# Order of v loads, partition groups and index scatters in an attention and mixture-of-experts kernel

## The chip, the cores and the metric

One core of one Trainium2 chip runs the whole program. The metric is the device time of one execution in microseconds, and lower is better.

## The reference

Two layers in a row. The attention takes q, k and v of 8 batches, 8 heads, 576 positions and 64 dimensions. It adds two softmax attentions: one over q, k and v averaged over groups of 4 positions (144 by 144 scores), its output repeated 4 times, and a local one in which a position sees the 3 before and the 3 behind it. The result, as 4608 tokens of 512 numbers, goes through a mixture of 8 experts, each token through the one with the largest gate:

```
logits = x @ w_gate + modality_bias[modality_id]
e_idx = np.argmax(logits, axis=1)
...
gate_w = probs[np.arange(N), e_idx]
for e in range(E):
    mask = e_idx == e
    h = np.maximum(x[mask] @ w1[e], 0.0)
    out[mask] = gate_w[mask, None] * (h @ w2[e])
```

## The kernel before, in words

**Attention.** It runs in N = 32 steps; step n does the heads 2·(n mod 4) and the next of batch n // 4. The order is a software pipeline written out by hand: a table PHASE gives each piece of work a place in steps, `call(n + p, ...)` collects all of them, and they are recorded in the order of these numbers. Each engine then works in that order (a piece that waits holds up all that stands behind it on its engine). In one step TensorE turns q and k (`tp`, L296), scores them (`sc` L364, `scd` L390), averages v (`vp` L284, once for two steps, so on one half of a batch's v), and multiplies by v (`avd` L460, `avl` L475). GpSimd (POOL) adds up q (`qe` L342, `qd` L346), adds a small number to the sums (`z` L412) and scales the two attention matrices (`le` L420, `de` L424); `scd` waits for `qd`, `avl` for `le` by way of a transposition (`lt`, L431) and a copy (`Pw`, L436).

**Loads.** All plain transfers are issued by SyncE (SP), in the same recorded order. A half batch of q and k is 4 transfers over 128 partitions (L252). A half batch of v is 4 transfers of 30 partitions each, one for each 32-partition group, in the order 0, 2, 1, 3 (L272; the last batch is cut once more, L271). v has two buffers, `vw` of even and of odd batches; a half of one is free when the products `avl` of the batch two before have read it. In before both halves of the next batch but one step are recorded together at 4·b − 1 + P["v"] and 0.8 steps later.

**Routing.** Nine or ten half tiles of tokens of a batch are turned back (`R`) and stored to a scratch `xs` in DRAM (`store`, L647): 4 transfers, one for each 32-partition group, in the order 0 to 3. Each token's place in its expert's list is worked out on VectorE (`pb` ends with the column `si`), and `st` (L653) writes 128 tokens' entries into the table `tab` with one indirect transfer from POOL; a batch has 4 or 5. Batches 0 to 3 (EB = 4) are "early": the first units of 512 tokens for the experts are made from them while the attention still runs. In before each scatter of batches 0 to 6 has a place of its own in the order, those of batch 6 by a rule of their own; those of batch 7 stand behind the attention.

**Experts.** Tokens are gathered by the table (L949, L957). w1 comes in chunks (`fetch`): for w1 4 transfers of 32 partitions and 128 KB each in the order 0 to 3 (L864), for w2 one of 128 partitions (L867). Chunks 0 to 3 of the first expert are loaded and split into a high and a low part while the attention ends: POOL casts chunk 0 and 1 (L888), at ws00 and ws10 of the table, between `z` and `qd` of two late steps, and chunks 2 and 3 behind the last `de`. Behind the attention come two units of 512 tokens, three of 1024, and three small ones; TensorE's float32 products in three passes (L1026, L1079) fill it from then on.

**A scheduler for what is not written out.** The pieces in `manual_schedule()` keep their order. Those recorded outside of it, as batch 7's routing under `high_priority()`, are put by a scheduler where it holds them to be ready, and that can be between pieces recorded earlier.

Of the kernel before, what the change touches and what calls it, by code (L numbers as in the profile page):

```python
# [23 lines left out]
B, H, S, D = 8, 8, 576, 64  # L24
# [18 lines left out]
EB = 4  # L43
# [42 lines left out]
def whole(pieces):  # L86

    while True:
        try:
            next(pieces)  # L90
        except StopIteration as x:
            return x.value
# [399 lines left out]
class Router:  # L492
# [147 lines left out]
    def store(s, b, t):  # L640

        n = min(2, s.t["G", b] - 2 * t)
        if n > 0:
            r0 = 128 * (s.t["t0", b] + 2 * t)
            R = s.t.pop(("R", b, t))
            for a in range(4):
                s.nc.sync.dma_start(s.xs[r0 : r0 + 128 * n, 128 * a : 128 * a + 128].rearrange("(i j) x -> j i x", j=32),  # L647
                                    R[32 * a : 32 * a + 32, : 4 * n].rearrange("p i k c -> p i (k c)"))

# [169 lines left out]
class Moe:  # L819
# [38 lines left out]
    def fetch(s, raw, e, c, quarters=False):  # L858
        nc = s.nc
        if c < 4:  # L860
            for i in range(4):
                x, y = (c, i) if quarters else (i, c)
                r = 256 * (x // 2) + 64 * (x % 2) + 128 * (y // 2) + 32 * (y % 2)
                nc.sync.dma_start(raw[32 * i : 32 * i + 32], s.w1[bass.ds(e, 1), r : r + 32, :].rearrange("o p f -> (o p) f"))  # L864
        else:
            c -= 4
            nc.sync.dma_start(raw.rearrange("p (f d) -> p f d", f=2),  # L867
                              s.w2[bass.ds(e, 1), 256 * c : 256 * c + 256, :].rearrange("o (f p) d -> p (o f) d", p=128))
# [226 lines left out]
class Large:  # L1095
# [69 lines left out]
    def first(s, hook):  # L1165
# [20 lines left out]
        for n, nm in enumerate("1256743"):  # L1186
            (wh, wl), (xh, xl) = s.t.pop((nm, "W")), s.t.pop((nm, "X"))
            acc, new = (Z, nm != "3") if nm in "253" else (X, nm == "1")
            for f in range(4):
                fs = slice(128 * f, 128 * f + 128)  # L1190
                for k in range(2):
                    for i, (a, x) in enumerate(((wh, xh), (wh, xl), (wl, xh))):
                        nc.tensor.matmul(acc[f], a[:, k, fs], x[:, k, :], start=new and k == i == 0, stop=k == 1 and i == 2,
                                         skip_group_check=True)
                t = X[f]
                if nm == "6":
                    if f == 0:
                        part = m.block("raw1", F32).rearrange("p (f t) -> p f t", f=4)
                    nc.scalar.copy(part[:, f], t)
                elif nm in "273":  # L1200
                    t = m.xp.tile([128, DM], F32, name="o", bufs=3)
                    if nm != "3":
                        nc.scalar.copy(t, X[f])
                    nc.vector.tensor_tensor(t, part[:, f] if nm == "3" else t, Z[f], op=ALU.add)  # L1204
                if late:
                    store(*late.pop())
                if nm in "2743":
                    late.append(({"2": 0, "7": 6, "4": 2, "3": 4}[nm], f, t))
                hook(n, f)
        store(*late.pop())  # L1210
        s.h = [[[H[i + j] for j in (0, 2)] for i in (0, 1)], [[H[i + j] for j in (4, 6)] for i in (0, 1)]]

# [5 lines left out]
def build(tc, q, k, v, mid, w_gate, bias, w1, w2, out):  # L1218
    nc = tc.nc
    with ExitStack() as ctx:  # L1220
# [10 lines left out]
        with ExitStack() as actx:  # L1231
            ectx = ExitStack()
            ro = Router(tc, ctx, C, ps, xs, tab, tables)
# [5 lines left out]
            at = Attention(tc, actx, ectx, C, ps, q, k, v)  # L1239
# [9 lines left out]
            N = 4 * B  # L1249
# [17 lines left out]
            def call(at, f, *args):  # L1267
                calls.append((at, len(calls), f, args))

            P = PHASE  # L1270
            parts = {"kT": "kT_", "Pw": "Pw_", "W": "store", "lm": "lm", "le": "le"}
            used = max(P["avl0"], P["avl1"])
# [3 lines left out]
            for nm, p in P.items():  # L1276
                if nm in FIXED or nm[:2] in SETUP:
                    continue
                f, i = (nm[:-1], int(nm[-1])) if nm[-1].isdigit() else (nm, 0)
                if f in batch:  # L1280
                    for b in range(B - 1):
                        at_ = 4 * b + p
                        if f == "st" and b == B - 2:
                            at_ = {2: max(N - 2 + P["nd"], 4 * b + P["pb"]) + 0.0001, 0: N - 1 + P["nl"] + 0.0001,
                                   3: N - 0.865 + P["nd"]}.get(i, N + 2.2)
                        call(at_, getattr(ro, parts.get(f, f)), b, i)
                else:
                    for n in range(0, N, 2 if f in ("vp", "vc", "tpt") or nm in ("qT1", "kT1", "kd1") else 1):
                        call(n + p, values if f == "X" else getattr(at, parts.get(f, f)), n, i)
            for b in range(B):  # L1290
                if b + 1 < B:
                    for j in range(2):
                        call(4 * b - 1 + P["v"] + 0.8 * j, at.load_v, b + 1, 4 * j)
            for h in range(3, N // 2):
                call(2 * h - 5 + P["qk"], at.load_qk, h // 2, h % 2)

# [57 lines left out]
            t = 4 * (EB - 1) + max(P[x] for x in P if x[:2] == "st") + 0.02  # L1354
# [7 lines left out]
                call(sorted(P[f"row{j}"] for j in range(4))[i], rows, 0, i)  # L1362
            free = N - 1 + max(P["scd"], P["sc0"], P["sc1"]) + 0.02

            w = max(t + 5, 4 * (B - 2) - 1 + used + 1.1 + 0.8)
            for c in range(4):
                call(w - 1.5 + 0.5 * c, wload, c)
            for c in range(2):
# [29 lines left out]
            b = B - 1  # L1398
            with tc.high_priority():
                for f, k in ((ro.lg, 2), (ro.LT, 2), (ro.lgt, 2), (ro.L, 2)):  # L1400
                    for i in range(k):
                        f(b, i)
                for f in ROUTE[:9] + ROUTE[10:12]:
                    getattr(ro, f)(b, 0)
                cnt = whole(ro.counts("m"))
                for f in ("pr", "pa", "pb"):
                    getattr(ro, f)(b, 0)
                for i in range(5):
                    ro.st(b, i)
            moe.after = ro.last_act, ro.last_dve  # L1410
            for i in range(5):
                ro.R(b, i)
# [7 lines left out]
        lists, Es, Ts, Rs, Xs, parts = {}, {}, {}, {}, {}, {}  # L1420

        N, written = len(order), ExitStack()
# [208 lines left out]
```

## Time and profile before

| | us |
|---|---|
| median of 3 runs | 677.1 (673.7 to 679.29) |
| the profiled execution | 672.38 |
| its span, first to last instruction | 670.7 |
| TensorE busy in the span | 633.4 |

The profile is of one execution. TensorE's busy share is a share of the span, with ends that are modelled; VectorE is DVE, ScalarE is ACT, GpSimd is POOL, SyncE's queue is SPq. In a timeline the brackets give the idle time of the engine ahead of an instruction and what ended it. [...]

### The profile page before, as it was taken

How to read it: one execution, taken by the hardware profiler on the slowest of the kernel's cores; microseconds unless marked ns; L12 is line 12 of the kernel's file. 1: busy time of each engine (PE TensorE's matmuls, PEld its weight loads, DVE VectorE, ACT ScalarE, POOL GpSimd, SP SyncE). 2: the span in 40 equal slices, each digit the busy share in tenths (PEclk: the TensorE clock that was granted, in tenths of full speed). 3: DMA queues.
4: the chain of work that ended last, by engine and by line, in shares of the span. 5: the costliest groups of instructions: out<-in, count | busy, mean ns of one | idle time of the engine just before them, and what ended most of it. 6: DMA issues, size and time to landing. Idle time of an engine off the chain costs nothing. (4 is left out here: it accounts for less than half of the span.)

```text
span 670.7 us, 16185 instructions
## 1 busy us (share of the span) xinstructions
PE 633.4 (94%) x5995; PEld 498.4 (74%) x5995; DVE 425.6 (63%) x897; ACT 386.8 (58%) x902; POOL 345.7 (52%) x414
## 2 busy tenths in 40 slices
PE   7799999899988769999999999999999999999996
PEld 4577677676756556887888888888888888889894
DVE  6678898699968574834435773676736967225550
ACT  4789999899979462413354743446424464335540
POOL 7635666557656665333039876498764740113102
PEclk9899999899989797999999999999999999999999
DMA  9999988997999968077002326233351244537701
GB/s 184 163 168 194 160 152 180 161 203 146 177 176 184 190 159 211 27 186 194 0 33 98 107 74 175 53 103 103 84 158 72 79 111 141 169 113 212 233 1 44
DMA packets 178011, 90.20 MB, mean 134 GB/s; under 512 B 144036, under 2 KB 162506, under 8 KB 177930
## 3 DMA queue, kind: packets, MB, share of 16 engines
q1 hardware_dynamic: 169994, 69.96, 49.0%
q0 software_dynamic: 7936, 19.18, 9.3%
q8 instruction: 48, 0.79, 0.6%
q14 instruction: 33, 0.27, 0.2%
HBM read 69.86 MB, written 19.51 MB: 133 GB/s over the span
## 5 line engine op out<-in xcount | busy, mean ns | idle before, releaser
L1079 PE MATMUL l<-V,H 128*128 128x512 f32 x804 | 190.4, 395 | 0.0
L1079 PEld LDWEIGHTS l<-V,H 128*128 128x128 f32 x804 | 150.3, 188 | 34.6
L957 POOL DMA_INDIRECT xg<-xs,m x64 | 74.7, 1167 | 19.2 <-issue 18.9
L1089 POOL DMA_INDIRECT out_dram<-o,tq x24 | 28.9, 1204 | 79.4 <-ACT o L1081 61.4
L1026 PE MATMUL l<-X,H 128*128 128x512 f32 (+1 forms) x264 | 58.8, 374 | 0.9 <-DVE X L999 0.9
L436 ACT COPY Pw<-lt 32x288 f32<-32x288 f32 x128 | 54.5, 426 | 5.3 <-DVE lt L431 3.8
L1081 ACT ACTIVATE o<-l,tq 128x512 f32<-128x512 f32 x24 | 16.5, 689 | 70.1 <-PE l L1079 45.1
L1026 PEld LDWEIGHTS l<-X,H 128*128 128x128 f32 x264 | 45.4, 192 | 10.9 <-issue 1.5
L653 POOL DMA_INDIRECT tab<-ig,si x36 | 38.4, 1066 | 15.5 <-DVE mhni L677 9.4
L475 PE MATMUL avl<-Pw,vw 128*64 128x96 f32 x768 | 42.3, 257 | 4.2 <-ACT Od L465 2.0
L1182 ACT ACTIVATE H<-o 128x512 fp32r<-128x512 f32 x36 | 22.8, 634 | 39.8 <-DVE o L1204 39.6
L1089 POOL DMA_INDIRECT out_dram<-o,tg x12 | 14.0, 1170 | 59.8 <-ACT o L1081 43.1
L412 POOL TENSOR_SCALAR z<-z 128x15 f32<-128x15 f32 x32 | 8.4, 261 | 68.0 <-ACT de L403 22.5
L475 PEld LDWEIGHTS avl<-Pw,vw 128*64 128x64 f32 x768 | 34.4, 141 | 9.9 <-ACT Od L465 3.7
L1031 ACT ACTIVATE H<-l 128x512 fp32r<-128x512 f32 x24 | 14.4, 599 | 46.9 <-PE l L1026 46.9
L328 ACT COPY kT<-tp 64x512 f32<-64x512 f32 x64 | 37.0, 578 | 4.4 <-DVE kd L336 2.8
L894 DVE TENSOR_TENSOR V<-raw,V 128x1024 fp32r<-128x1024 f32 x23 | 34.3, 1509 | 7.4 <-ACT V L888 7.4
L364 PE MATMUL sc<-kT,qT 128*24 128x64 f32 x1536 | 35.2, 223 | 3.7 <-ACT kT L328 3.3
L403 ACT ACTIVATE de<-scd,dm 128x144 f32<-128x144 f32 x96 | 35.6, 373 | 3.3 <-DVE dm L395 2.4
L894 DVE TENSOR_TENSOR H<-raw,H 128x1024 fp32r<-128x1024 f32 x12 | 15.0, 1256 | 34.5 <-ACT H L888 19.4
L1032 DVE SCALAR_TENSOR_TENSOR H<-l,H 128x512 fp32r<-128x512 f32 x24 | 16.6, 690 | 30.5 <-ACT H L1031 30.4
L390 PE MATMUL scd<-kd,qd 64*64 64x144 f32 x384 | 32.7, 306 | 1.0 <-POOL qd L346 1.0
(276 smaller groups left out, 1450.5 us busy)
## 6 DMA issues: line engine op xcount, KB each, us to landing
raw<-in_moe_w_dram SPq DMA_DIRECT2D x112, 128.0 KB
raw<-in_moe_w_dram SPq DMA_DIRECT2D x28, 512.0 KB
vw<-in_v_dram SPq DMA_DIRECT2D x60, 180.0 KB
qt<-in_q_dram SPq DMA_DIRECT2D x30, 288.0 KB
kt<-in_k_dram SPq DMA_DIRECT2D x30, 288.0 KB
xs<-R SPq DMA_DIRECT2D x56, 128.0 KB
xs<-G SPq DMA_DIRECT2D x8, 128.0 KB
xg<-xs,m POOLq DMA_INDIRECT x64, 2.9
```

Source lines behind the costliest of these rows:

```text
L328: s.nc.scalar.copy(s.kB[r, g, a, PAD + 64 * g : PAD + 64 * g + 512], p[r])
L364: s.nc.tensor.matmul(p[32 * j : 32 * j + SUB, 2 * i : 2 * i + 2, :], qT[:, q0 : q0 + SUB], kB[:, :, q0 : q0 + WIN], start=False, stop=(i = ...
L390: s.nc.tensor.matmul(p[r, c, :], qd[r, 40 * c : 40 * c + 64], kd[r, :], start=True, stop=True, skip_group_check=True)
L403: s.nc.scalar.activation(x, s.t["scd", n][:, c].rearrange("p (k x) -> p k x", k=NB), AF.Exp, bias=m[:, c : c + 1], accum_out=s.t["z", n][: ...
L436: s.nc.scalar.copy(s.Pw[n % NPW][r, :, j, :SUB], s.t["lt", n][r, :, :SUB])
L475: s.nc.tensor.matmul(p[64 * a : 64 * a + 64, c], vw[:, NB * (4 * (hp // 2) + hp % 2 + 2 * a) + k, :], Pw[:, 2 * k + a], start=True, stop=T ...
L653: i = nc.gpsimd.indirect_dma_start(out=s.tab[:, :], out_offset=bass.IndirectOffsetOnAxis(ap=C.si[:, t : t + 1], axis=0), in_=C.ig[:, t, :] ...
L894: (nc.gpsimd if turn == 4 else nc.vector).tensor_tensor(lo, raw, hi.bitcast(F32), op=ALU.subtract)
L957: s.nc.gpsimd.indirect_dma_start(out=R[l].rearrange("p h (i x) -> p (h i) x", i=4)[:, i, :], out_offset=None, in_=s.xs.rearrange("n (a x) ...
L1026: nc.tensor.matmul(p[:, f % n, :], a[:, fs], x[:, k, :N], start=(k == 0 and i == 0), stop=(k == 3 and i == 2))
L1079: nc.tensor.matmul(p, l, x[:, f % 2, :], start=(f == 0 and i == 0), stop=(f == 7 and i == 2))
L1089: nc.gpsimd.indirect_dma_start(out=s.out[:, :], out_offset=bass.IndirectOffsetOnAxis(ap=T[:, h, 0:1], axis=0), in_=o, in_offset=None, boun ...
```

## The change

Three edits. `store` and `fetch` go through the groups in the order 0, 2, 1, 3. Scatters of batches 4 to 6 lose their places in the order and are recorded behind the attention with those of batch 7, under `high_priority()`. The halves of v are recorded apart, each 0.02 steps behind the last reader of its buffer (`used` is the later of avl0 and avl1), which is 2.2 steps earlier for the first half and 1 step earlier for the second; the place `w` of the first weights is 0.3 steps earlier.

```diff
-            for a in range(4):
+            for a in (0, 2, 1, 3):
                 s.nc.sync.dma_start(s.xs[r0 : r0 + 128 * n, 128 * a : 128 * a + 128].rearrange("(i j) x -> j i x", j=32),
...
-            for i in range(4):
+            for i in (0, 2, 1, 3):
                 x, y = (c, i) if quarters else (i, c)
...
                     for b in range(B - 1):
-                        at_ = 4 * b + p
-                        if f == "st" and b == B - 2:
-                            at_ = {2: max(N - 2 + P["nd"], 4 * b + P["pb"]) + 0.0001, 0: N - 1 + P["nl"] + 0.0001,
-                                   3: N - 0.865 + P["nd"]}.get(i, N + 2.2)
-                        call(at_, getattr(ro, parts.get(f, f)), b, i)
+                        if f != "st" or b < EB:
+                            call(4 * b + p, getattr(ro, parts.get(f, f)), b, i)
...
-                        call(4 * b - 1 + P["v"] + 0.8 * j, at.load_v, b + 1, 4 * j)
+                        call(4 * b - 3 + used + 2 * j + 0.02 if b else P["v"] + 0.8 * j - 1, at.load_v, b + 1, 4 * j)
...
-            w = max(t + 5, 4 * (B - 2) - 1 + used + 1.1 + 0.8)
+            w = max(t + 5, 4 * (B - 2) - 1 + used + 1.6)
...
-                for i in range(5):
-                    ro.st(b, i)
+                for x in range(EB, B):
+                    for i in range(5):
+                        ro.st(x, i)
```

On SP, in the middle of the attention (batches 4 and 5; `qt` and `kt` a half of q and k, `vw` v, `xs<-R` a store). Before:

```order
L252 DMA qt<-in_q_dram 128x9x64 x2
L252 DMA kt<-in_k_dram 128x9x64 x2
L647 DMA xs<-R 32x8x128 x4
L272 DMA vw_155<-in_v_dram 30x24x64 x8
L252 DMA qt<-in_q_dram 128x9x64 x2
L252 DMA kt<-in_k_dram 128x9x64 x2
L647 DMA xs<-R 32x8x128 x4
L252 DMA qt<-in_q_dram 128x9x64 x2
L252 DMA kt<-in_k_dram 128x9x64 x2
L647 DMA xs<-R 32x8x128 x4
L272 DMA vw_156<-in_v_dram 30x24x64 x8
```

After, the same stretch:

```order
L272 DMA vw_155<-in_v_dram 30x24x64 x4
L252 DMA qt<-in_q_dram 128x9x64 x2
L252 DMA kt<-in_k_dram 128x9x64 x2
L647 DMA xs<-R 32x8x128 x4
L272 DMA vw_155<-in_v_dram 30x24x64 x4
L252 DMA qt<-in_q_dram 128x9x64 x2
L252 DMA kt<-in_k_dram 128x9x64 x2
L647 DMA xs<-R 32x8x128 x4
L272 DMA vw_156<-in_v_dram 30x24x64 x4
L252 DMA qt<-in_q_dram 128x9x64 x2
L252 DMA kt<-in_k_dram 128x9x64 x2
L647 DMA xs<-R 32x8x128 x4
```

The first half of a batch's v has moved ahead of one half of q and k and one store; the second half stands where it stood.

On SP, at the last batch, from its second half of q and k on (`raw` is chunk 0 of the first expert's w1, four transfers of it to a chunk). Before:

```order
L252 DMA qt<-in_q_dram 128x9x64 x2
L252 DMA kt<-in_k_dram 128x9x64 x2
L647 DMA xs<-R 32x8x128 x4
L272 DMA vw_156<-in_v_dram 30x24x64 x4
L864 ISA
L864 DMA raw_4138<-in_moe_w_dram 32x1024
L864 ISA
L864 DMA raw_4138<-in_moe_w_dram 32x1024
```

After:

```order
L252 DMA qt<-in_q_dram 128x9x64 x2
L252 DMA kt<-in_k_dram 128x9x64 x2
L647 DMA xs<-R 32x8x128 x4
L272 DMA vw_156<-in_v_dram 30x24x64
L271 DMA vw_156<-in_v_dram 30x64
L272 DMA vw_156<-in_v_dram 30x23x64
L271 DMA vw_156<-in_v_dram 30x64
L272 DMA vw_156<-in_v_dram 30x23x64
L271 DMA vw_156<-in_v_dram 27x64
L272 DMA vw_156<-in_v_dram 30x23x64
L864 ISA
L864 DMA raw_4102<-in_moe_w_dram 32x1024
```

The first half of the last v has gone from here to a place ahead of these rows, and the second half, which stood behind chunks 0 and 1, now stands ahead of chunk 0.

On POOL, at the scatters of batch 5 (`L653`), from the first of them on; `L949` is a gather for the first unit, `L888` the cast of chunk 0. Before:

```order
L653 DMA tab<-ig,si 41472x2
L342 TENSOR_TENSOR qe<-qT 128x288
L653 DMA tab<-ig,si 41472x2
L949 DMA xg<-xs,tg_3674 128x512
L412 TENSOR_SCALAR z<-z 128x5x3
L346 TENSOR_TENSOR qd<-qe 128x144
L420 TENSOR_TENSOR le_168<-le_168,zr 128x12x30
L653 DMA tab<-ig,si 41472x2
L424 TENSOR_TENSOR de_171<-de_171,zr 128x18x24
L653 DMA tab<-ig,si 41472x2
L342 TENSOR_TENSOR qe<-qT 128x288
L412 TENSOR_SCALAR z<-z 128x5x3
```

After:

```order
L653 DMA tab<-ig,si 41472x2 x5
L342 TENSOR_TENSOR qe<-qT 128x288
L949 DMA xg<-xs,tg_3674 128x512
L412 TENSOR_SCALAR z<-z 128x5x3
L346 TENSOR_TENSOR qd<-qe 128x144
L420 TENSOR_TENSOR le_168<-le_168,zr 128x12x30
L424 TENSOR_TENSOR de_171<-de_171,zr 128x18x24
L342 TENSOR_TENSOR qe<-qT 128x288
L412 TENSOR_SCALAR z<-z 128x5x3
L888 CAST H_4602<-raw_4102 128x1024
L346 TENSOR_TENSOR qd<-qe 128x144
```

The scheduler has put the five scatters of batch 5 in one run into the attention, where the first of them stood. Batch 4's four stand in the same way in one run where its first one stood, and batch 6's four in one run behind the last `de` but one, where its first one stood; only batch 7's five stand behind the attention, as before.

## Rows read from the trace of the kernel before

**Rows 1.** The page: granted clock and DMA share in 40 slices
```profile
PEclk9899999899989797999999999999999999999999
DMA  9999988997999968077002326233351244537701
```

**Rows 2.** Windows by stage: stretch, length, busy time by engine, clock, DMA share, GB/s
```profile
45.00:223.00 178.00, 164.08 (x3140) 121.15 (x3138) 144.70 (x440) 158.67 (x500) 105.39 (x160) 0.98 0.93 174
223.00:258.00 35.00, 28.40 (x415) 20.90 (x413) 26.41 (x64) 20.92 (x64) 24.75 (x27) 0.84 0.80 165
258.00:661.00 403.00, 402.06 (x1888) 329.66 (x1887) 224.36 (x307) 176.74 (x250) 188.07 (x163) 1.00 0.39 112
```

**Rows 3.** Timeline of TensorE where it waits for v, start, length, idle before
```profile
128.58 1.70 PE L284 MATMUL vp<-vw,pool 128*32 128x256 f32 x12 [1.91 <-DMA vw<-in_v_dram]
...
187.03 1.93 PE L284 MATMUL vp<-vw,pool 128*32 128x256 f32 x12 [3.11 <-DMA vw<-in_v_dram]
...
221.15 1.93 PE L284 MATMUL vp<-vw,pool 128*32 128x256 f32 x12 [5.37 <-DMA vw<-in_v_dram]
...
224.83 1.71 PE L390 MATMUL scd<-kd,qd 64*64 64x144 f32 x12 [0.59 <-POOL qd L346]
```

**Rows 4.** Timeline of SP's queue, 150 to 226 us
```profile
176.86 10.18 SPq L272 DMA_DIRECT2D vw<-in_v_dram  x8
...
209.37 6.70 SPq L272 DMA_DIRECT2D vw<-in_v_dram  x4
216.27 5.04 SPq L864 DMA_DIRECT2D raw<-in_moe_w_dram  x8
221.56 0.35 SPq L272 DMA_DIRECT2D vw<-in_v_dram  x1
...
225.29 0.34 SPq L272 DMA_DIRECT2D vw<-in_v_dram  x1
```

**Rows 5.** Timeline of POOL, batches 4 and 5's scatters and the cast of chunk 0
```profile
172.84 1.06 POOL L653 DMA_INDIRECT tab<-ig,si  x1 [0.16 <-DVE lm L371]
...
185.27 1.05 POOL L653 DMA_INDIRECT tab<-ig,si  x1 [0.15 <-ACT qT L314]
...
204.78 1.10 POOL L653 DMA_INDIRECT tab<-ig,si  x1 [0.16 <-DVE lm L371]
...
213.09 1.01 POOL L653 DMA_INDIRECT tab<-ig,si  x1 [0.17 <-issue]
...
214.90 0.26 POOL L412 TENSOR_SCALAR z<-z 128x15 f32<-128x15 f32 x1
223.34 1.04 POOL L888 CAST H<-raw 128x1024 fp32r<-128x1024 f32 x1 [8.19 <-DMA raw<-in_moe_w_dram]
```

**Rows 6.** Windows as in rows 2, of short stretches
```profile
45.00:62.00 17.00, 17.00 (x344) 12.57 (x344) 15.24 (x51) 16.48 (x55) 8.41 (x15) 1.00 1.11 197
...
149.00:157.00 8.00, 7.00 (x132) 5.31 (x125) 7.87 (x21) 7.10 (x24) 5.92 (x11) 1.00 0.67 113
290.00:292.00 2.00, 2.00 (x10) 1.64 (x9) 0.19 (x1) 0.00 (x0) 0.99 (x1) 1.00 0.79 238
303.00:305.00 2.00, 2.00 (x10) 1.63 (x9) 1.37 (x2) 1.42 (x2) 1.67 (x2) 1.00 1.06 396
...
218.01:234.78 16.77, 13.04 (x177) 8.82 (x179) 9.74 (x22) 8.03 (x25) 11.01 (x13) 0.80 1.10 190
```

**Rows 7.** The table's scatters, 145 to 157 us, and landing of those of 160 to 217 us
```profile
L653 POOL DMA_INDIRECT tab<-ig,si x4: 1004/1028/1054, 145.7 to 153.9; - x4
...
DMA to landing us min/median/max: 5.6/6.1/8.9
```

**Rows 8.** SP's stores of 70 to 215 us: duration min, median, max, first, last
```profile
L647 SPq DMA_DIRECT2D xs<-R x48: 430/479/2475, 74.5 to 207.8; - x48
```

**Rows 9.** Timeline of the attention's end: POOL, ACT, TensorE
```profile
246.62 1.04 POOL L888 CAST H<-raw 128x1024 fp32r<-128x1024 f32 x1
...
250.22 1.09 PE L981 MATMUL xt<-ident,xg 128*128 128x128 f32 x8 [2.94 <-ACT PdT L453]
```

## The prediction

> **What bounds the kernel now.** I read the windows by stage first. From 258 us to the end TensorE is busy 402 of 403 us at full clock [rows 2], and the change alters none of its products there. So the end moves as the start of that stretch moves, and only the attention ahead of it can win or lose time. There the page's slices show the DMA engines at nine tenths or more almost all the way to 235 us [rows 1], a share of 0.93 from 45 to 223 us [rows 2]. TensorE is busy 164 of those 178 us. Two limits lie close together, so I asked next where TensorE stops. Three times it waits for v, ahead of the averages of batches 4, 6 and 7: 1.91, 3.11 and 5.37 us, together 10.4 us [rows 3]. Around the third the granted clock is 0.80 on the mean of 16.77 us [rows 6]; with levels of 1.00 and 0.50 that is 6.7 us at half clock, 3.4 us of work. The page's slices dip at the two before as well [rows 1].
>
> SP's own timeline says why v is late. SP issues without a pause, and a transfer's issue takes about as long as its data: the eight of v for batch 6 take 10.18 us from 176.86 us, and TensorE gets the first four at 187.03 us [rows 4, 3]. The four of batch 7 start at 209.37 us, are issued by 216.07 us and let TensorE go at 221.15 us, 5.1 us later. So the queue stands about 5 us deep behind SP: it is the queue's total content, not the moment at which SP is allowed to issue, that decides when something lands.
>
> The last thing that the queue makes wait is chunk 0 of the weights. POOL is ready for its cast from 215.2 us on and starts it at 223.34 us, after 8.19 us for the raw weights [rows 5]. `qd` stands behind that cast, and TensorE's `scd` at 224.83 us behind `qd` [rows 3]. Everything from there to 258 us is one chain of steps.
>
> **Part 1, halves of v.** By the order, the first half of v of each batch goes ahead of one half of q and k and one store. It then lands some 8 to 10 us earlier, by SP's rows two groups of transfers, and that covers 1.91, 3.11 and 5.37 us. No byte is added or taken away, so what was overtaken lands later: an odd half of q and k moves back by a half of v, 4 to 6 us. I expect some of the waits for v to come back as waits for q and k at `tp`. What matters for the end is chunk 0. Before, the second half of the last v stood behind chunks 0 and 1; now it stands ahead. Its seven transfers took from 221.56 to 225.63 us [rows 4], so chunk 0 lands **4.1 us** later if the queue moves as it did. The 5.37 us wait goes, but TensorE then waits at `scd` a few instructions later, for POOL, which waits for chunk 0: the stall changes its name. `w`'s 0.3 steps hide behind a queue that is late anyway: nothing.
>
> **Part 2, scatters.** The text puts them behind the attention, but the order shows runs of four, five and four inside it. What they cost the queue: from 45 to 62 us, without one, it moves 197 GB/s; from 149 to 157 us, among the four scatters of 145.7 to 153.9 us, 113 GB/s [rows 6, 7]. That is 3.4 us lost of 8, 0.85 us for each. The fifth scatter of batch 5 now runs ahead of chunk 0: +0.9 us, if the loss goes by their number. If it goes by the time in which any is on its way, 6.1 us each [rows 7], the runs win: batch 4's were on their way from 172.84 to 191.4 us and batch 5's from 204.78 to 219.2 us [rows 5]; in runs at 1.2 us each (1.05 and a gap of 0.16) these are 9.7 and 10.9 us instead of 18.5 and 14.4, so 12.3 us less at 43% loss, −5.3 us. Bounds −5.3 and +0.9; I take **−2.0**, the middle, since no row has scatters so close beside loads.
>
> On POOL the run of five holds up `qe`, `z` and `qd` of its step: five times 1.2 us where two scatters stood, about 4 us late. At this place POOL waited 8.19 us for chunk 0 in the next step [rows 5], and that wait is the cover: nothing, or 4 us if chunk 0 came early. The run of four for batch 4 delays its step by about 2 us in the stretch in which the queue is late: nothing. The last run stands ahead of the last step's `z` and `de`, where one scatter stood ahead of `z` and one between `le` and `de`: 4.8 us from the same start instead of 1.2, of which `z` had 1.6 us of idle; by `de` the delay is 1.0 us. The cast of chunk 2 at 246.62 us and TensorE's 2.94 us wait ahead of 250.22 us [rows 9] move with it: **+1.1 us**, between 0 and 2.2 (the delay of `z`).
>
> **Part 3, the groups.** 48 stores of 74.5 to 207.8 us carry 5.8 MB (40 of 128 KB, 8 of 64 KB) [rows 8]. Weights in groups of 32 partitions in the old order move at 238 GB/s, weights over 128 partitions at 396 [rows 6]. If the new order gave stores the second rate for the first, they would take 14.6 us of the queue instead of 24.2: −9.6 us. If groups stay one behind the other, nothing. v, which has the order 0, 2, 1, 3 already, goes at 145 GB/s (8 times 180 KB in 10.18 us) [rows 4], so the order alone brings no high rate; I take **−2.5**, a quarter. Chunk 0's 512 KB: −0.9 to 0 by the same rates, I take **−0.2**.
>
> [...] No row here shows stores in the new order.
>
> **The sum.** Chunk 0: 4.1 − 2.0 − 2.5 − 0.2 = −0.6 us; the end of the attention +1.1. Together **+0.5 us**, no change that can be told. The profiled execution goes from 672.4 to 672.9 us; it lies 4.7 us under the median of the runs, so the median goes from 677.1 to about 678. Steps of 1% (6.8 us) are about what a measurement of this kernel can tell from no change.
>
> **Rivals.**
> Faster: the queue really moves faster. For it speak the two rates of rows 6 and the loss beside scatters; against it the share of 0.93, which leaves little idle, and v's rate. With −9.6 for the stores and −2.0 for the runs, chunk 0 would be 8 us early. The gain ends where v and POOL's own order end it: the 5.37 and 0.59 us waits and 3.4 us of clock, so −9.4, and +1.1 at the end: 664 us, 669 as a median. [...]
>
> Slower: chunk 0 behind the last v. Place: POOL's cast of chunk 0, with `qd` behind it and TensorE behind that. Price: 4.1 us, 0.9 us for the fifth scatter, 1.1 us at the end, and up to 1.7 us, half of the 3.4, for a longer half clock: +7.8, so 680 us, 685 as a median. It decides as soon as neither stores nor runs relieve the queue. Rows 5 speak for it, 8.19 us in which chunk 0 was the last to come; against it, that nothing of the queue's content has been added.
>
> Also possible: the waits for v were the true limit and chunk 0 comes as early as they allow, because TensorE's progress and not the queue holds back SP. Then 10.4 us and at least 3.4 us of clock go: 659 us. Rows 4 speak against it: SP is late, not waiting. I count it with the faster case.
>
> **How the numbers follow.** Forecast, within a few us of 678: 0.52. Faster: 0.26, with a few of its outcomes within 1%. Slower: 0.22, about half at over 1%, and from the forecast's own upper end (+4.1 without relief) some more. This gives faster by over 1% 0.25, within 1% 0.53, slower by over 1% 0.22. The range 666 to 688 reaches from the faster rival's end, a little beyond, to somewhat past the slower one; the likeliest case's own is 673 to 683.
>
> **What would show it.** Right: the waits at `vp` for v are gone or under 1 us; POOL's wait for the raw weights is still there, at some 8 to 12 us, with its cast within 3 us of 223; waits for `qt` or `kt` at `tp` of late steps; DMA share near 0.93 up to the cast. Wrong: a cast before 217 us, or a GB/s clearly above 174 from 45 us to the cast (stores or runs relieved the queue); a cast past 227 us; idle time of TensorE at `scd` of the run of five, which would mean that its 4 us have no cover.

## The result, and the profile after

The changed kernel takes 682.58 us in the median of 20 executions (678.84 to 691.54), the kernel before 675.96 us beside it (20 executions, 671.35 to 685.71). The ratio is 1.0107, with a 95% interval of 1.0082 to 1.0132: it is about 7 us slower. The ratio leaves out executions more than 1.5% above the fastest of their kernel (one of after, three of before), which is why it gives 7.2 us and the medians 6.6. The two profiled executions lie 12.1 us apart (684.50 and 672.38 us), since before's is 3.6 us under its median and after's 1.9 us over its own; the traces therefore show about 5 us more than there is to explain.

TensorE's granted clock (in tenths of full speed) and the DMA share of after, in 40 slices of the page, answer to [rows 1]:

```profile
PEclk9899999998998897999999999999999999999999
DMA  9989788889999943449103226214162233536701
```

The clock dips in other slices than before, the last time (7) at the end of the attention as before, and the DMA engines are busy for seven tenths or more up to the fourteenth slice. The windows of after (stretch, length, busy time by engine, clock, DMA share, GB/s), to be held against [rows 2]:

```profile
45.00:223.00 178.00, 165.51 (x3067) 121.98 (x3055) 142.35 (x433) 154.82 (x488) 105.62 (x160) 0.95 0.93 170
...
229.00:264.00 35.00, 26.21 (x374) 19.74 (x374) 24.47 (x59) 19.85 (x61) 23.30 (x26) 0.77 0.47 128
262.00:673.00 411.00, 408.70 (x1928) 334.23 (x1927) 225.85 (x313) 179.08 (x256) 187.79 (x163) 0.99 0.38 112
```

The queue carries 170 GB/s where it carried 174, so no relief shows, and the clock there is 0.95 for 0.98. The last 35 us of the attention run at a clock of 0.77 instead of 0.84, and the expert part is again nearly all product. So most of the time was lost ahead of it: the attention's last `avl` ends at 266.8 us on TensorE, in before at 256.9, which is 9.9 of the 12.1 us. The other 2.2 lie in the expert part, where single executions of the ten kernels without scatters moved behind the attention differ by more (412.8 to 417.1 us from that `avl` to the end).

TensorE's timeline of after, at its waits of over 1 us from 150 to 256 us (start, length, idle before and what ended it):

```profile
158.52 1.08 PE L296 MATMUL tp<-ident,kt 128*128 128x128 f32 x4 [2.73 <-DMA kt<-in_k_dram]
...
182.38 0.53 PE L364 MATMUL sc<-kT,qT 128*24 128x64 f32 x19 [1.12 <-issue]
...
213.63 0.31 PE L364 MATMUL sc<-kT,qT 128*24 128x64 f32 x4 [1.13 <-issue]
...
231.40 1.71 PE L390 MATMUL scd<-kd,qd 64*64 64x144 f32 x12 [4.45 <-POOL qd L346]
...
253.91 0.65 PE L981 MATMUL xt<-ident,xg 128*128 128x128 f32 x4 [3.99 <-ACT PdT L453]
```

The three waits for v of [rows 3] are gone. A wait for `kt` has come, and the largest one stands at `scd` for `qd`, 4.45 us where [rows 3] has 0.59; `scd` itself is 6.6 us later (231.40 for 224.83). SP's and POOL's timelines of after say why; they answer to [rows 4] and [rows 5]:

```profile
212.48 4.86 SPq L647 DMA_DIRECT2D xs<-R  x4
217.44 0.47 SPq L272 DMA_DIRECT2D vw<-in_v_dram  x1
...
222.81 0.33 SPq L272 DMA_DIRECT2D vw<-in_v_dram  x1
223.32 8.83 SPq L864 DMA_DIRECT2D raw<-in_moe_w_dram  x15
```

```profile
229.91 1.04 POOL L888 CAST H<-raw 128x1024 fp32r<-128x1024 f32 x1 [5.52 <-DMA raw<-in_moe_w_dram]
```

SP reaches chunk 0 at 223.32 us, before at 216.27. Of these 7.05 us, 5.88 are the second half of the last v (217.44 to 223.32), and 1.2 us is what stands ahead of it. The cast follows at 229.91 us for 223.34.

### The profile page after: what moved, and what is told of

The parts are those of the page before. It is cut to its first block, busy times and chain, and to the rows that moved or that the text cites. A ratio compares the mean times of both kernels' runs of the same rounds, so it can differ in the third digit from the quotient of the medians.

```text
span 682.8 us, 16190 instructions
## 1 busy us (share of the span) xinstructions
PE 641.5 (94%) x5995; PEld 504.4 (74%) x5995; DVE 425.0 (62%) x897; ACT 387.1 (57%) x902; POOL 344.5 (50%) x414
## 5 line engine op out<-in xcount | busy, mean ns | idle before, releaser
L957 POOL DMA_INDIRECT xg<-xs,m x64 | 76.7, 1199 | 19.2 <-issue 18.3
L1089 POOL DMA_INDIRECT out_dram<-o,tq x24 | 27.4, 1143 | 78.7 <-ACT o L1081 68.9
L364 PE MATMUL sc<-kT,qT 128*24 128x64 f32 x1536 | 39.8, 230 | 8.4 <-issue 4.9
L653 POOL DMA_INDIRECT tab<-ig,si x36 | 36.9, 1026 | 20.7 <-DVE mhni L677 13.1
L364 PEld LDWEIGHTS sc<-kT,qT 128*24 128x24 f32 x1536 | 26.5, 106 | 19.1 <-issue 12.4
L1143 DVE TENSOR_TENSOR G<-X,G 128x1024 fp32r<-128x1024 f32 x15 | 23.2, 1552 | 22.4 <-ACT G L1142 22.4
L894 DVE TENSOR_TENSOR V<-raw,V 128x1024 fp32r<-128x1024 f32 x23 | 32.1, 1412 | 7.2 <-ACT V L888 7.1
```

Source lines behind the costliest of these rows:

```text
L364: s.nc.tensor.matmul(p[32 * j : 32 * j + SUB, 2 * i : 2 * i + 2, :], qT[:, q0 : q0 + SUB], kB[:, :, q0 : q0 + WIN], start=False, stop=(i = ...
L653: i = nc.gpsimd.indirect_dma_start(out=s.tab[:, :], out_offset=bass.IndirectOffsetOnAxis(ap=C.si[:, t : t + 1], axis=0), in_=C.ig[:, t, :] ...
L894: (nc.gpsimd if turn == 4 else nc.vector).tensor_tensor(lo, raw, hi.bitcast(F32), op=ALU.subtract)
L957: s.nc.gpsimd.indirect_dma_start(out=R[l].rearrange("p h (i x) -> p (h i) x", i=4)[:, i, :], out_offset=None, in_=s.xs.rearrange("n (a x) ...
L1089: nc.gpsimd.indirect_dma_start(out=s.out[:, :], out_offset=bass.IndirectOffsetOnAxis(ap=T[:, h, 0:1], axis=0), in_=o, in_offset=None, boun ...
```

## The experiments

Each kernel was timed against the kernel before on the same chip; the times in us are the ratio's distance from 1 times before's median there (671.0 to 676.0 us). "Cast" is the start of POOL's cast of chunk 0 in the one profiled execution, "rest" the span less that.

| run | v | scatters of batches 4 to 6 | groups | ratio, 95% interval | us | cast | rest |
|---|---|---|---|---|---|---|---|
| before | old | old | old | 1 | 0 | 223.3 | 447.4 |
| after | early | runs | new | 1.0107 (1.0082 to 1.0132) | +7.2 | 229.9 | 452.9 |
| g_groups | old | old | new | 0.9973 (0.9929 to 1.0017) | -1.8 | 227.1 | 445.7 |
| s_scatters | old | runs | old | 1.0079 (1.0035 to 1.0123) | +5.3 | 222.7 | 448.7 |
| v_halves | early | old | old | 1.0076 (1.0043 to 1.0109) | +5.1 | 229.4 | 447.1 |
| a_old_scatters | early | old | new | 1.0071 (1.0034 to 1.0108) | +4.8 | 231.6 | 447.2 |
| s_last_run | old | last run only | old | 1.0011 (0.9979 to 1.0043) | +0.7 | 222.7 | 450.1 |
| s_first_runs | old | first two runs only | old | 0.9974 (0.9945 to 1.0002) | -1.8 | 224.5 | 449.9 |
| a_late_half | early but last half | runs | new | 1.0007 (0.9973 to 1.0040) | +0.5 | 228.5 | 447.5 |
| a_late_half_old_scatters | early but last half | old | new | 1.0026 (1.0000 to 1.0053) | +1.7 | 224.4 | 447.9 |
| s_behind | old | behind | old | 0.9887 (0.9847 to 0.9927) | -7.6 | 215.7 | 443.2 |
| a_behind | early | behind | new | 1.0075 (1.0037 to 1.0113) | +5.0 | 221.8 | 450.6 |
| a_late_half_behind | early but last half | behind | new | 0.9973 (0.9940 to 1.0005) | -1.8 | 219.3 | 450.8 |
| s_behind_groups | old | behind | new | 1.0011 (0.9977 to 1.0046) | +0.7 | 219.4 | 458.4 |

**One edit at a time.** g_groups has the two loops over (0, 2, 1, 3) and nothing else.

```diff
-            for a in range(4):
+            for a in (0, 2, 1, 3):
...
-            for i in range(4):
+            for i in (0, 2, 1, 3):
```

> The kernel before with the order 0, 2, 1, 3 of the partition groups for stores and weights, and nothing else. Theory Q (the new order gives the queue nothing, so my -2.5 us was never there): within 1 us of before, POOL's cast of chunk 0 within 1 us of 223.3 us, and the 48 stores issued in about 0.48 us each as before. Rival (neighbouring groups relieve each other, and the gain is hidden in the changed kernel by its other edits): chunk 0 cast 2.5 to 9.6 us earlier and the kernel 2 us or more faster.

Measured: 0.9973, not to be told from 1. The 48 stores of g_groups on SP, as in [rows 8]:

```profile
L647 SPq DMA_DIRECT2D xs<-R x48: 432/473/3735, 75.8 to 210.6; - x48
```

A median of 473 ns stands where [rows 8] has 479, and added up the 48 take 37.8 us in both kernels. The window from 45 to 223 us has 170 GB/s for 174, and the cast came later, not earlier. The queue shows no relief. That the cast stands 3.7 us later than before's fits neither expectation: so much can a single execution differ. A gain of the size of my 2.5 us lies inside the interval of the time, but nothing in the trace carries it.

s_scatters has the third hunk of the change and the loop over `range(EB, B)`.

```diff
...
-                        call(at_, getattr(ro, parts.get(f, f)), b, i)
+                        if f != "st" or b < EB:
+                            call(4 * b + p, getattr(ro, parts.get(f, f)), b, i)
...
-                for i in range(5):
-                    ro.st(b, i)
+                for x in range(EB, B):
+                    for i in range(5):
+                        ro.st(x, i)
```

> The kernel before with the edit of the scatters alone: batches 4 to 6 in runs of four, five and four. Theory R (a run of scatters holds POOL and slows the other engines' issue; the first two runs are covered by waits for v, the last by nothing): 3 to 5 us slower than before, with TensorE's step ahead of the xt products at the attention's end late by about 4 us, and chunk 0's cast within 1.5 us of 223.3 us. Rival 1 (only a delayed chunk 0 makes the changed kernel slower): the same as before within 1.5 us. Rival 2 (the runs relieve the queue, my term of -2.0 us): chunk 0 is cast 2 us or more earlier.

Measured: 1.0079, a loss as theory R has it, so rival 1 is out. Of the 12 times five lie from 672.4 to 674.8 us and seven from 678.3 to 683.8; the profiled execution (673.1) is one of the five, so its trace doesn't show the 5.3 us. Its cast (222.7 us) speaks against rival 2. ACT's timeline at the last run, whose four scatters stand at 239.13 to 244.04 us on POOL:

```profile
244.23 0.40 ACT L453 COPY PdT<-pdt 96x288 f32<-96x288 f32 x1 [3.46 <-issue]
```

`PdT` copies `pdt`, which TensorE had finished by 240.40 us. ACT stood until the run was over. This stall is thus in one of the five faster executions, so by itself it does not make the loss.

v_halves has the edit of `load_v` and of `w`.

```diff
-                        call(4 * b - 1 + P["v"] + 0.8 * j, at.load_v, b + 1, 4 * j)
+                        call(4 * b - 3 + used + 2 * j + 0.02 if b else P["v"] + 0.8 * j - 1, at.load_v, b + 1, 4 * j)
...
-            w = max(t + 5, 4 * (B - 2) - 1 + used + 1.1 + 0.8)
+            w = max(t + 5, 4 * (B - 2) - 1 + used + 1.6)
```

> The kernel before with the earlier halves of v alone. Theory C (chunk 0 behind the second half of the last v costs what that half takes in the queue): the waits for v at vp are gone, chunk 0's cast moves from 223.3 to 228 to 230 us, and the kernel is 4 to 6 us slower than before. Rival (the delay of chunk 0 needs the scatters' runs as well, which slow the queue and the issue ahead of it; alone, the vanished waits for v pay for it): within 2 us of before or faster, cast at 221 to 226 us.

Measured: 1.0076, theory C to the letter. TensorE and POOL in v_halves, the two rows that answer to `scd` in [rows 3] and the cast in [rows 5]:

```profile
230.91 1.70 PE L390 MATMUL scd<-kd,qd 64*64 64x144 f32 x12 [8.05 <-POOL qd L346]
```

```profile
229.42 1.04 POOL L888 CAST H<-raw 128x1024 fp32r<-128x1024 f32 x1 [10.63 <-DMA raw<-in_moe_w_dram]
```

The 5.37 us for v have become 8.05 us for chunk 0. SP spent 4.08 us on the half here (220.06 to 224.14 us).

a_old_scatters is the changed kernel with the scatters' hunk of s_scatters taken back.

> The changed kernel with the scatters back at the places that they had before: halves of v and groups alone. Theory R: about 4 us faster than the changed kernel (678 to 679 us), because the run of four ahead of the last steps' work is gone, with the cast of chunk 0 still late at 228 to 230 us. Rival 1 (chunk 0 alone is the loss): 682 to 683 us, as the changed kernel. Rival 2 (the runs had relieved the queue): chunk 0's cast later than 230 us and over 683 us.

Measured: 1.0071. Beside after's 1.0107 it is some 2.4 us better than the changed kernel, less than theory R's 4 us, and the two intervals meet, so that rival 1 is not excluded. The cast, 231.6 us, is 1.7 us later than after's, which is rival 2's sign; its time is not (677.4 us in the median). Elsewhere the sign changes: with runs the cast is 0.6 us earlier than before's in s_scatters, 1.2 us later in s_first_runs, and 4.1 us later in a_late_half than in a_late_half_old_scatters. A relief by the runs is not shown.

**The last run, the last half, and scatters really behind.** s_last_run moves batch 6's scatters alone.

```diff
...
+                        if f != "st" or b < B - 2:
+                            call(4 * b + p, getattr(ro, parts.get(f, f)), b, i)
...
+                for x in range(B - 2, B):
```

> The kernel before with batch 6's four scatters alone in a run behind the last de but one; those of batches 4 and 5 stay at their old places. The kernel with all three runs came out 1.0079 of before (+5.3 us). Theory R (the last run has no cover: while it is issued, ACT and TensorE stop as well as POOL): +3 to +5 us, nearly all of it, with ACT idle 3 us or more ahead of PdT and TensorE ahead of xt. Rival (the first two runs cost the time, in the queue or as broken issue of sc, and the last one only takes over waits that before has at the same place): within 1.5 us of before.

Measured: 1.0011, so theory R fell: the last run alone costs nothing that can be told. POOL in s_last_run:

```profile
246.49 0.91 POOL L424 TENSOR_TENSOR de<-de,zr 128x432 f32<-128x432 f32 x1
```

The same `de` in before:

```profile
245.77 0.92 POOL L424 TENSOR_TENSOR de<-de,zr 128x432 f32<-128x432 f32 x1
```

TensorE in s_last_run:

```profile
251.73 1.54 PE L981 MATMUL xt<-ident,xg 128*128 128x128 f32 x6 [3.40 <-ACT PdT L453]
```

Here no wait for a product of TensorE ends with the run. `de` starts 0.7 us later than in before (I had worked out 1.0), and TensorE waits 3.40 us ahead of `xt` where [rows 9] has 2.94.

s_behind is the kernel before with the scatters held behind the last split of the weights on POOL (`lo4` is that instruction). They stand behind all of POOL's work for the attention, while TensorE still has its last products.

```diff
...
+                        if f != "st" or b < EB:
+                            call(4 * b + p, getattr(ro, parts.get(f, f)), b, i)
...
+                for x in range(EB, B):
+                    for i in range(5):
+                        with tc.issue_after(moe.lo4.ins):
+                            ro.st(x, i)
```

> The kernel before with the scatters of batches 4 to 6 really behind the attention: 13 in a row on POOL behind the last split of the weights, so none stands in the attention from batch 4 on. If scatters inside the attention take 0.85 us each of the queue (as estimated from the windows of before), the nine ahead of chunk 0 bring it 4 to 8 us earlier, its cast to 215 to 220 us, and the end of the attention 3 to 5 us earlier; the table is then late by up to eight scatters of 1.3 us, about 10 us, for the gathers of the next unit. Theory G (those gathers are needed soon behind the attention): the gain is lost there, 0 to 8 us slower than before. Rival (TensorE has work of the first units for longer than that): 3 to 5 us faster. If the cast stays at 223 us, scatters don't load the queue.

Measured: 0.9887 from six executions, 660.6 to 665.6 us, all under the lowest of the kernel before (666.3), and more than the 3 to 5 us of the rival. Window, SP's rows of v for batches 6 and 7, and cast of s_behind:

```profile
45.00:223.00 178.00, 166.08 (x3192) 123.36 (x3183) 149.17 (x448) 159.56 (x508) 102.41 (x159) 0.97 0.94 182
```

```profile
176.73 7.08 SPq L272 DMA_DIRECT2D vw<-in_v_dram  x8
...
205.67 2.73 SPq L272 DMA_DIRECT2D vw<-in_v_dram  x4
```

```profile
215.72 1.04 POOL L888 CAST H<-raw 128x1024 fp32r<-128x1024 f32 x1 [4.93 <-DMA raw<-in_moe_w_dram]
```

The window has 182 GB/s for 174, SP issues these transfers of v in 7.08 and 2.73 us where [rows 4] has 10.18 and 6.70, and the cast comes 7.6 us earlier. Gone from ahead of the cast are eight scatters and not nine, as the expectation has it: batch 5's fifth stands behind it in before.

```profile
227.54 1.06 POOL L653 DMA_INDIRECT tab<-ig,si  x1 [0.16 <-issue]
```

That is 0.95 us for each, where the estimate from [rows 6, 7] was 0.85. So without scatters the queue is faster, about as estimated. POOL is also free of eight times 1.2 us (1.05 and a gap of 0.16 in [rows 5]); no run separates that from the queue, but the cast still waited for its weights (4.93 us) and not for POOL. The rest of the span is 4.2 us shorter as well, which no run explains.

a_late_half puts one half of v back into the changed kernel.

```diff
-                        call(4 * b - 3 + used + 2 * j + 0.02 if b else P["v"] + 0.8 * j - 1, at.load_v, b + 1, 4 * j)
+                        at_ = 4 * b - 3 + used + 2 * j + 0.02 if b else P["v"] + 0.8 * j - 1
+                        if b == B - 2 and j:
+                            at_ = 4 * b - 1 + P["v"] + 0.8
+                        call(at_, at.load_v, b + 1, 4 * j)
```

> The changed kernel with the second half of the last batch's v back behind chunks 0 and 1, where before had it; every other half of v stays early. v halves alone were 5.1 us slower than before, with the cast of chunk 0 at 229.4 us. Theory C (that half ahead of chunk 0 is the price of part 1): the cast at 222 to 225 us and 4 to 6 us faster than the changed kernel, so 4 to 6 us slower than before less the same, about +1 to +3 us. Rival (the halves overtaken by v, or the earlier halves of all batches, delay the queue as a whole): cast later than 227 us, and no more than 1.5 us faster than the changed kernel.

Measured: 1.0007, 6.7 us better than the changed kernel by the two ratios. The cast was expected at 222 to 225 us and stands at 228.5; but the profiled execution took 677.65 us, the longest of its 12 (median 671.41), so that the time shows that this half costs the loss, and this trace does not show it at chunk 0.

a_late_half_old_scatters has both, that half and the old scatters.

> The same, and the scatters back at their old places: what is left of the change are the groups and the early halves of v up to batch 6 and of the first half of batch 7. Theories C and R together: the two losses are gone and the waits at vp with them, so 0 to 4 us faster than before. Rival (early v only moves the wait to kt or qd): the same as before within 1 us.

Measured: 1.0026, a hair slower than before and not faster, as the theories had it. The cast, 224.4 us, is 7.2 us earlier than in a_old_scatters, from which only the place of that half differs. Its trace shows the rival: 4.13 and 4.68 us at `tp` for `kt` in the place of the waits for v.

```profile
156.73 0.63 PE L296 MATMUL tp<-ident,kt 128*128 128x128 f32 x4 [4.13 <-DMA kt<-in_k_dram]
...
221.17 1.09 PE L296 MATMUL tp<-ident,kt 128*128 128x128 f32 x4 [4.68 <-DMA kt<-in_k_dram]
```

**What the parts do together.** s_first_runs is s_scatters with batch 6 left at its old places.

```diff
-                        call(at_, getattr(ro, parts.get(f, f)), b, i)
+                        if f != "st" or b < EB or b == B - 2:
+                            call(at_, getattr(ro, parts.get(f, f)), b, i)
...
-                for i in range(5):
-                    ro.st(b, i)
+                for x in (EB, EB + 1, B - 1):
+                    for i in range(5):
+                        ro.st(x, i)
```

> The kernel before with batch 4's four and batch 5's five scatters in runs, as the change puts them; batch 6's stay at their old places. All three runs were 5.3 us slower than before, batch 6's alone 0.7 us (interval -1.4 to +2.9). Theory F (the first two runs cost the time: products of sc are issued in pieces while a run goes on, and the clock falls to its lower level for it): +3 to +6 us, half clock behind the runs. Rival (it takes all three runs: each delay alone is still covered, and only their sum is not): within 1.5 us of before.

Measured: 0.9974. Theory F fell as well: neither the first two runs (-1.8) nor the last (+0.7) has the cost that all three have (+5.3). The rival would remain, that only the sum of all three is not covered; but a_late_half has all three runs too and is no slower than a_late_half_old_scatters (+0.5 and +1.7). So the cost belongs to s_scatters and not to the runs as such; what makes it is not shown.

The last three put the scatters really behind (the edit of s_behind) in the changed kernel (a_behind), in a_late_half (a_late_half_behind) and in g_groups (s_behind_groups).

> The changed kernel with the scatters of batches 4 to 6 really behind the attention. In the kernel before this gave -7.6 us (ratio 0.9887), with chunk 0's cast at 215.7 us. Theory S (scatters inside the attention load the queue ahead of chunk 0, wherever in it they stand): the cast 6 to 9 us earlier than the changed kernel's 229.9 us, and 8 to 12 us faster than the changed kernel, so 1 to 5 us faster than before. Rival (with chunk 0 behind the last v, v and not the scatters holds it up): no more than 4 us faster than the changed kernel, slower than before.

> The same, and the second half of the last v behind chunks 0 and 1 as in before. Theory: chunk 0 comes as early as in the kernel before with its scatters behind (215 to 218 us), and the waits for v are gone as well, so 6 to 10 us faster than before. Rival (the early halves of v only pass their wait on to q and k at tp): as the kernel before with its scatters behind or up to 3 us slower, so -5 to -8 us.

> The kernel before with the scatters really behind the attention and the groups in the order 0, 2, 1, 3; v as before. Groups alone were -1.8 us (interval -4.8 to +1.1). If they relieve the queue: 8 to 11 us faster than before, with stores issued faster than 0.48 us each in the median. If they give nothing: 7 to 8 us faster, as the scatters behind alone.

Measured: 1.0075 (seven executions), 0.9973 and 1.0011. Their casts came 8.1 us earlier than the changed kernel's, 9.2 us earlier than a_late_half's and 7.6 us earlier than g_groups': theory S holds for the cast. The time did not follow: a_behind is where its rival has it (2.2 us better than the changed kernel, slower than before), and the other two miss what was expected of them either way. The rest of the span is 450.6, 450.8 and 458.4 us where s_behind has 443.2, so it was given back behind the cast.

The traces show where. The experts' first `H` on ACT needs a group of TensorE's products `l`, the last of which stand in one row of eight. That row of TensorE and ACT's `H`, first in s_behind and then in a_behind:

```profile
250.16 2.12 PE L1028 MATMUL l<-X,H 128*128 128x512 f32 x8
252.09 0.60 ACT L1033 ACTIVATE H<-l 128x512 fp32r<-128x512 f32 x1 [6.52 <-PE l L1028]
```

```profile
256.87 2.12 PE L1028 MATMUL l<-X,H 128*128 128x512 f32 x8
268.05 0.60 ACT L1033 ACTIVATE H<-l 128x512 fp32r<-128x512 f32 x1 [16.11 <-remote]
```

In s_behind `H` starts before the row's end, in the middle of the run of 13 (242.82 to 259.10 us). In a_behind it starts 9.1 us behind the row's end and 2.2 us behind that of the run (249.56 to 265.83 us). In a_late_half_behind and s_behind_groups, with runs to 262.79 and 262.47 us, it is the same:

```profile
266.49 0.60 ACT L1033 ACTIVATE H<-l 128x512 fp32r<-128x512 f32 x1 [17.20 <-remote]
```

```profile
271.64 0.60 ACT L1033 ACTIVATE H<-l 128x512 fp32r<-128x512 f32 x1 [22.66 <-remote]
```

These two starts are 9.3 and 15.0 us behind the end of the same row of eight. The three delays of 9.1, 9.3 and 15.0 us stand beside rests that are 7.4, 7.6 and 15.2 us longer than s_behind's, so in these executions the loss lies here. In s_behind_groups, whose profiled execution is 4.5 us above its median, DVE and TensorE stood first, its 13 scatters being at 246.19 to 262.47 us on POOL:

```profile
265.08 0.46 DVE L486 TENSOR_TENSOR X<-avl,Od 128x288 f32<-128x288 f32 x1 [14.11 <-remote]
```

```profile
250.91 0.72 PE L475 MATMUL avl<-Pw,vw 128*64 128x96 f32 x12
...
265.60 1.81 PE L526 MATMUL lg<-X,wg 128*32 128x320 f32 x9 [8.96 <-issue]
```

DVE's `X` needs `avl`, which is over at 251.63 us by TensorE's row, and Od, which ACT has done by 248.98; it starts at 265.08, when the scatters are through, and TensorE's `lg` waits for it. In s_behind, with the same instructions beside a run of 13, DVE waited for nothing there.

## Why the prediction was right or wrong

I forecast 678 us, no change that can be told, in a range of 666 to 688. The time is in the range and at the upper end of the likeliest case (673 to 683), but the case that came is the slower rival: chunk 0 behind the last v, at +7.8 us, a median of 685. Measured are +7.2 us, a ratio over 1%, to which I had given 0.22. So that the time lies in the likeliest case's own range is luck: what was to make that case, reliefs as large as the loss, did not come. That the rival's +7.8 is so near is in part luck too, since 1.7 of it are for a longer stretch at half clock (in before the clock is 0.50 from 222 to 227 us), and no run shows that term by itself.

**Chunk 0, +4.1 us: right in place, and the cause.** With the second half of the last v ahead of chunk 0 the kernel is slower, with it behind it is within 2 us of before, whatever the scatters do: a_old_scatters against a_late_half_old_scatters +4.8 and +1.7, after against a_late_half +7.2 and +0.5, a_behind against a_late_half_behind +5.0 and -1.8. That is 3.1, 6.7 and 6.8 us, 5.5 in the mean; in the first pair the intervals meet, in the others they don't. The casts go with it: 229.4 to 231.6 us in v_halves, after and a_old_scatters, 222.7 to 227.1 us in the five kernels with v as before and no scatters behind the attention, 224.4 in a_late_half_old_scatters; only a_late_half's long execution (228.5) does not fit. SP spent 4.08 us on the half in v_halves, 5.88 in after, 7.19 in a_old_scatters and 3.46 in a_behind. In v_halves the chain from the cast to the end did not change: the rest of the span is 447.1 us, in before 447.4. That the clock is not what delays the cast shows in v_halves too, with 0.98 from 45 to 223 us as in before. That the wait for v would only change its name, to `scd`, was right.

**The reliefs, -2.0, -2.5 and -0.2 us: the step that failed.** I had set them against the 4.1 us, the one as the middle of bounds of -5.3 and +0.9, the next as a quarter of -9.6, since no row showed scatters side by side with loads or stores in the new order. Neither appears in the queue: 170 GB/s in g_groups and in after, 48 stores of 37.8 us in all in g_groups as in before (45.2 us in after), casts at 227.1 us with the groups alone and at 222.7 to 224.5 us with runs alone. The rate of 396 GB/s in [rows 6], from which the -9.6 came, was not that of weights alone either: 0.18 of the 0.79 MB in that window are gathers. The -9.6 us did not come: the stores of g_groups take 473 ns in the median for 479, and its interval of time ends at -4.8 us. For the scatters the bound +0.9, a loss that goes by their number, fits better: runs, which shorten the time in which any is on its way (batch 5's five are issued from 207.94 to 214.13 us in after, from 204.78 to 228.60 us in before), show no relief, and s_behind gains 0.95 us for each of the eight that it takes from ahead of the cast. The ninth alone, by which the changed kernel differs, is too little to be told in a cast.

**The end of the attention, +1.1 us (0 to 2.2): right without a stall, too small with one.** From the end of the last `scd` to that of the last `avl` TensorE's rows have 16.7 us in before and 15.5 to 17.2 us in the five other kernels with batch 6's scatters at their old places. In s_last_run and a_late_half they have 18.0 and 17.8 us, 1.3 and 1.1 more than before; in after and s_scatters 19.1 and 19.7, which is 2.4 and 3.0 more. In after the run of 247.69 to 252.60 us did more than delay POOL, by ACT's timeline:

```profile
253.46 0.40 ACT L453 COPY PdT<-pdt 96x288 f32<-96x288 f32 x1 [4.11 <-remote]
```

ACT's `PdT` starts 0.86 us behind the run's end, for a `pdt` that TensorE had finished by 249.33 us, and TensorE's 3.99 us ahead of `xt` end with it; ahead of the next `xt` it then waits 1.57 us, where [rows 9] has 2.94. That such a stall makes up a part of the 7.2 us is likely and not shown: between a_old_scatters and after there are 2.4 us, less than their intervals.

**The run of five, costed at nothing: right.** I had named idle time of TensorE at its step as the sign that it has no cover. Its `sc` did break into pieces, eight from 210.04 to 216.19 us for a group that takes 0.54 us. The pauses between them add up to 3.6 us. But chunk 0 came later than that: `scd` waited 4.45 us in after and 8.05 in v_halves, where no run stood, which is 3.6 us less. So the run was covered. In s_first_runs this run and the one ahead of it cost nothing either (-1.8 us).

**The forecast signs.** Gone waits at `vp`, a wait for `kt` at `tp` (2.73 us) and a DMA share of 0.93 came. POOL's wait for the raw weights was 5.52 us and not 8 to 12, since the run of five had held POOL, and the cast stood past 227 us, which I had named as a sign that the forecast is wrong. The change's text says that the scatters stand behind the attention. They don't, and where they do (a_behind) the kernel is still 5.0 us slower than before. That does not clear the place where they stand: in a_behind the cast came 8.1 us earlier, and the wait of the experts' first `H` took most of it back.

**What stays open.** s_behind is the one version that beats both kernels, by six executions; why a run of 13 holds up `H` in the three kernels with the new groups and not there, and why three runs cost in s_scatters what neither part does, is not settled. The measurement of s_behind was not repeated.

## What to carry to other kernels

When a load is moved ahead, look at the last place where it can overtake something: the halves of v could go early at little cost (and without a gain), all but the last, which then stood ahead of the transfer that the whole end waited for. A loss that a row shows should not be set off against reliefs that no row shows; as rivals with their own chances these would have left +5 us as the forecast. And where a scheduler places what the text only moves, read the order that comes out, then try the place that was meant.

## What the runs showed that I had not expected

Beside small indirect scatters in a row other engines stood still. In five kernels an engine got a finished product of TensorE only when the run was over: 0.86 us behind its end in after (4.11 us of wait), 0.19 us in s_scatters (3.46), 2.61 us in s_behind_groups (14.11), 2.2 us in a_behind (16.11) and 3.7 us in a_late_half_behind (17.20). In s_last_run, a_late_half and s_behind runs of four and of 13 passed without it. What makes the engine wait the trace doesn't show: it calls the releaser "remote" or "issue". The run of five in after has a milder form, `sc` in eight pieces mostly some 0.72 us apart; in a_late_half, beside the same run (210.94 to 217.11 us), `sc` comes whole, 24 products in 0.54 us.

That scatters of 128 tiny entries take 0.85 us each of a queue that others fill was an estimate, and it held roughly: in four pairs of kernels that differ in nothing else the cast came 7.6 to 9.2 us earlier with the scatters behind the attention, 0.90 to 1.02 us for each of the eight or nine ahead of it (each from one execution; for a_late_half a long one).
